# A planned order chosen anew: early norms on GpSimd, mask products in two turns only

## The chip, the cores and the metric

One core of a Trainium2 chip runs the kernel. The metric is the device time in microseconds of one execution; the kernel before takes 620.43 us in the median of three runs (619.21 to 622.95).

## What is computed

Three layers follow one another, all in float32, for 4 batches of 576 tokens with 8 heads of width 64 (512 channels):

- windowed attention: `scores = q k^T / 8`, masked to the last 64 positions, softmax, `attn v`;
- a gated layer: `h = relu(x w_in)`, split in `u` and `v`; `v` is normalised over its channels; `gated = u * (w_spatial v_n + b)`; then `gated w_out`;
- a token and channel mixer: `u = x + w_tok2^T relu(w_tok1^T x)`, `out = u + relu(u w_ch1) w_ch2`.

A full float32 product is made of three faster ones: each operand is split in a high part (a cast) and a low part (the rest), and high·high, high·low and low·high are summed in PSUM. The weights arrive as 64-bit floats and are turned into float32 on the chip (a scaling on ScalarE, two integer operations on VectorE) before they are split.

## The kernel before

The first part of the kernel, up to about 220 us, is attention and most of the gated layer. It runs in 18 **turns** of 128 query rows (two turns collect the tail rows of two batches, 0 and 9). Nothing in it is ordered by hand: the function `plan` lists steps, each with an engine, a rank, a cost in us, the steps that it follows (`after`), and the buffers that it takes and gives (`take`, `give`); class `Steps` plays a simple model of the core in Python while the program is built. It takes next, among the steps that could start soonest, the one of the lowest rank, and writes its instructions. The engines then run in that written order, each with its own queue, and wait on semaphores for what the other engines owe. The costs therefore fix the order and nothing else.

The steps of turn n, with the names that this text uses:

- **Lq, Lv**: SyncE issues the loads of queries and keys (640 KB; 768 KB in the tail turns) and values (512 KB). Two turns' buffers each.
- **S** (`scores`, PE): 32 small products into two PSUM banks `sp` (four exist). In turns below `MASK_PE`, here 6, two bf16 products of an identity with the mask (L278, step **K** in this text) go ahead of them, so that the mask is already in the sum.
- **M** (`smax`, DVE, in two halves g of four heads): with the mask in the sum one reduction gives the maxima (L294, L301). In the other turns four custom instructions (L297) subtract from the mask, write the result to SBUF and leave the maxima, and the PSUM bank is free after M, not after X.
- **X** (`sexp`, ACT): four exponentials per half (L306), from PSUM or from SBUF, as M left them.
- **N** (`snorm`, DVE): sum plus epsilon, reciprocal (L314, L315, 128x4 each), and the multiplication of the half by it (L316, 128x512).
- **T** (PE): four transposes (L488) into a bank `sp`; **C** (ACT): the copy to SBUF (L489).
- **V** (`att_pv`, PE), then **xh** (ACT) and **xl** (DVE): the two parts of the layer's input.
- **v** (PE, 12 products) with its norm and split (`norm_parts`: relu and casts on ACT, statistics and low part on DVE, the inverse root on GpSimd, L375 and L376); after each third turn four **u** products; **s**, the spatial products, with their DVE eviction **G** (L406).

The weight `w_in` comes in eight pieces of 512 KB, four for v and four for u (`w_part`): load (SyncE) into a part of U, **wd** (ACT, L136) into a PSUM bank `mm`, **wo** (DVE, L439 and L440), **wh** (ACT, L443), **wl** (DVE, L445). The piece holds one of only three banks `mm` from wd to wl; the products v, u, s and one V of a pair use the same three. The first v needs all four v pieces.

SyncE issues nearly all loads in one queue. The first fourteen stand in a fixed list: q0, wv0, q1, wv1, v0, wv2, wv3, q2, v1, wu0, q3, wu1, wu2, wu3 (q: a turn's Lq, v: its Lv).

Work of the later layers (the pieces of `w_ch2`, names `craw`, `cx`, `raw`, `scr`; those of `w_out`, names `craw`, `val`) has the highest rank numbers and fills what the engines have left. `w_out` may start only after the last xl. Behind the plan, the rest of the kernel is written in order, with loads `k<-in_w_t` on the same SyncE queue.

Of the kernel before, what the change touches and what calls it, by code (L numbers as in the profile page):

```python
# [22 lines left out]
SCALE = 0.125  # L23
WN = 256
XW = 384
MASK_PE = 6
PB = 3
REST = 4
PAD = 0
PAIRS = 4  # L30
DOWN = 2.0 ** -112
SIGN = -2.0 ** 32

# [5 lines left out]
class Steps:  # L39
# [4 lines left out]

    def __init__(self, **room):
        self.room = {k: [0.0] * n for k, n in room.items()}
        self.clock, self.done, self.open, self.lines = {}, {}, [], {}
# [50 lines left out]
def tile_kernel(ctx, tc, qT, kT, kE, v, w_in, wsT, b_sp, w_out, w_t1, w_t2, w_c1, w_c2, outT):  # L98
# [328 lines left out]
    def w_part(raw, src, hi, lo, cols):  # L427
# [16 lines left out]
        yield  # L444
        nc.vector.tensor_tensor(out=lo, in0=v3, in1=f(hi), op=ALU.subtract)  # L445

    def wu_part(ft):
        fs = slice(128 * ft, 128 * ft + 128)
        return w_part(U[:, ft, :1024], w_in[:, fs].rearrange("(k p) c -> p k c", p=P), wi_h[:, :, fs], wi_l[:, :, fs], 128)
# [10 lines left out]
    def plan():  # L460
# [11 lines left out]
        def attend(n):  # L472
# [8 lines left out]
            def turned(g):  # L481
# [7 lines left out]
                copies[n, g] = lambda: nc.scalar.copy(out=PT[0][:, 4 * g:4 * g + 4, :], in_=pt)  # L489

            for g in range(2):
                S.add(("M", n, g), "DVE", 1 + n / 100, 0.95, lambda g=g: smax(n, g), after=[("S", n)], give=free * (n >= MASK_PE))
                S.add(("X", n, g), "ACT", 2 + n / 100, 1.65, lambda g=g: sexp(n, g), after=[("M", n, g)], give=free * (n < MASK_PE), hold=1.54)
                S.add(("N", n, g), "DVE", 1 + n / 100, 1.15, lambda g=g: snorm(n, g), after=[("X", n, g)], hold=1.05)
                S.add(("T", n, g), "PE", 1 + n / 100, 0.65, lambda g=g: turned(g), after=[("N", n, g)], take=free + ["PT"] * (g == 0), give=["pb"] * g, line=("T", n), hold=0.45)
                S.add(("C", n, g), "ACT", 1, 0.6, lambda g=g: copies.pop((n, g))(), after=[("T", n, g)], give=free, hold=0.49)
# [6 lines left out]

        def score(n, after, line):
            S.add(("S", n), "PE", 0, 1.2 + 0.6 * (n < MASK_PE), lambda: scores(n), after=after + [("Lq", n), "ident"],
                  take=[] if after else ["sp", "sp", "pb"], give=["qk"], hold=1.0 + 0.6 * (n < MASK_PE), line=line)

        def block(ns):

# [14 lines left out]
            take = ["xo"] + ["mm"] * (len(ns) - 1) + ["XT"] * sum(its[m][1] % 3 == 0 for m in ns) + ["sp", "sp", "pb"] * len(ahead)  # L524
            for m in ns:
                S.add(("V", m), "PE", 0, 1.25, lambda m=m: product(m), after=[("V", n)] if m > n else need,
                      take=take if m == n else [], give=["v", "PT"], hold=1.05, line=("B", n))
            for m in ahead:
                score(m, [("V", n)], ("B", n))
            for m in ns:  # L530
                S.add(("xh", m), "ACT", 0, 0.6, lambda m=m: xhigh(m), after=[("V", m)], hold=0.49)
                S.add(("xl", m), "DVE", 0, 0.7, lambda m=m: xlow(m), after=[("xh", m)], give=["mm" if m > n else "xo"], hold=0.6)

        def xhigh(n):
            p, i = its[n]
# [9 lines left out]
        def v_work(p, i):  # L545
# [12 lines left out]
            def part():  # L558
                next(g["it"], 0)

            S.add(("v", n), "PE", 10, 2.9, product, after=[("xl", n)] + [("wl", "v", k) for k in range(4)], take=["mm"], hold=2.75, line="work")
            S.add(("R", n), "ACT", 1.5, 0.6, relu, after=[("v", n)], take=["vf"], give=["mm"], hold=0.49)
            S.add(("bn", n), "DVE", 2, 0.9, part, after=[("R", n)])
            S.add(("rs", n), "POOL", 0, 1.0, part, after=[("bn", n)])
            S.add(("ts", n), "DVE", 2, 0.56, part, after=[("rs", n)])
            S.add(("hi", n), "ACT", 4, 0.6 if i else 2.2, part, after=[("ts", n)])
            S.add(("lo", n), "DVE", 3, 0.7 if i else 1.3, part, after=[("hi", n)], give=["vf"])

        def u_work(p, c, ft):
            g = {}  # L570

            def product():
                g["ps"] = bank(psmm, "mm")
                uv_u_mm(p, c, ft, g["ps"])

            S.add(("u", p, c, ft), "PE", 10, 2.25, product, after=[("xl", 9 * p + 3 * c + k) for k in range(3)] + [("wl", "u", ft)],
                  take=["mm"], give=["XT"] * (ft == 3), hold=2.09, line="work")
            S.add(("E", p, c, ft), "ACT", 1.5, 0.5 if c == 2 else 0.72, lambda: uv_u_out(p, c, ft, g["ps"]), after=[("u", p, c, ft)], give=["mm"])

        def s_work(b, d, c0):  # L580
            p = b // 2
# [2 lines left out]
            def product():  # L584
# [4 lines left out]
            S.add(("s", b, d, c0), "PE", 10, 2.0, product, after=tiles + [("ws", k, c0) for k in range(6)], take=["mm"], hold=1.86, line="work")  # L589
            S.add(("G", b, d, c0), "DVE", 0.5, 0.47, lambda: spatial_out(b, d, c0, g["ps"]),  # L590
                  after=[("s", b, d, c0)] + [("E", p, c, d) for c in range(2 + b % 2)], give=["mm"], hold=0.4)

        def w_load(kind, k):
            it = (wv_part if kind == "v" else wu_part)(k)

            def part():
                next(it, 0)

            S.add(("wL", kind, k), "SP", 0, 0, part, hold=0.47, kb=512, line="SP")
            S.add(("wd", kind, k), "ACT", 1.8 if kind == "v" else 2.5, 0.7, part, after=[("wL", kind, k)], take=["mm"], hold=0.6)  # L600
            S.add(("wo", kind, k), "DVE", 0.8 if kind == "v" else 2.5, 1.25, part, after=[("wd", kind, k)])
            S.add(("wh", kind, k), "ACT", 1.8 if kind == "v" else 2.5, 0.6, part, after=[("wo", kind, k)], hold=0.49)
            S.add(("wl", kind, k), "DVE", 0.8 if kind == "v" else 2.5, 0.7, part, after=[("wh", kind, k)], give=["mm"], hold=0.6)

        def ws_load(k, c):
            rows = P if k < 4 else 64
# [7 lines left out]
            S.add(("wh", k, c), "ACT", 3, 0.45, part, after=[("Lw", k, c)], hold=0.35)  # L614
            S.add(("ws", k, c), "DVE", 2.5, 0.45, part, after=[("wh", k, c)], give=["raw"], hold=0.38)

        def fetch_words(name, src, after, rank, line):

# [92 lines left out]
        for fn, *a in ((load_queries, 0), (w_load, "v", 0), (load_queries, 1), (w_load, "v", 1), (load_values, 0), (w_load, "v", 2), (w_load, "v", 3),  # L711
                       (load_queries, 2), (load_values, 1), (w_load, "u", 0), (load_queries, 3), (w_load, "u", 1), (w_load, "u", 2), (w_load, "u", 3)):
            fn(*a)
        for k in (0, 1):
            score(k, [], ("S", k))
# [594 lines left out]
```

## Time and profile before

| | |
|---|---|
| runs | 619.21, 620.43, 622.95 us |
| profiled execution | 621.39 us, span 619.5 us |
| granted TensorE clock, mean | 0.991 |
| PE busy | 600.2 us (97%) |
| DVE busy | 472.6 us (76%) |
| ACT busy | 352.7 us (57%) |
| POOL (GpSimd) busy | 114.7 us (19%) |
| DMA | 108.05 MB, mean 174 GB/s |

Busy shares are means over the whole span. The page's slices of 15.5 us show PE at four tenths in the first slice and at nine or more in nearly all others, and the clock in tenths at 8 in the first two slices and 9 or more (full) after. So what the first turns do has to be read in its own stretch. An idle time is named with the engine that ended it.

### The profile page before, as it was taken

How to read it: one execution, taken by the hardware profiler on the slowest of the kernel's cores; microseconds unless marked ns; L12 is line 12 of the kernel's file. 1: busy time of each engine (PE TensorE's matmuls, PEld its weight loads, DVE VectorE, ACT ScalarE, POOL GpSimd, SP SyncE). 2: the span in 40 equal slices, each digit the busy share in tenths (PEclk: the TensorE clock that was granted, in tenths of full speed). 3: DMA queues.
4: the chain of work that ended last, by engine and by line, in shares of the span. 5: the costliest groups of instructions: out<-in, count | busy, mean ns of one | idle time of the engine just before them, and what ended most of it. 6: DMA issues, size and time to landing. Idle time of an engine off the chain costs nothing.

```text
span 619.5 us, 12149 instructions
## 1 busy us (share of the span) xinstructions
PE 600.2 (97%) x4396; PEld 560.6 (90%) x4396; DVE 472.6 (76%) x1066; ACT 352.7 (57%) x889; POOL 114.7 (19%) x145
## 2 busy tenths in 40 slices
PE   4999999999999989999999999999999999999997
PEld 2678899889988989788988999999999999999997
DVE  5998878968888836586278778888875989866982
ACT  5996786766777532674344454546443557544540
POOL 3000202302422200041025212140011140011320
PEclk8899999999999999999999999999999999999999
DMA  8956356866565652415200524665534674444752
GB/s 325 342 187 188 124 198 228 262 225 223 203 203 180 229 179 69 137 57 167 84 34 35 170 69 169 221 224 168 184 126 173 230 234 159 153 137 170 237 197 77
DMA packets 49812, 108.05 MB, mean 174 GB/s; under 512 B 4948, under 2 KB 17496, under 8 KB 49752
## 3 DMA queue, kind: packets, MB, share of 16 engines
q1 hardware_dynamic: 49752, 107.27, 51.2%
q8 instruction: 35, 0.57, 0.4%
q14 instruction: 25, 0.20, 0.1%
HBM read 86.81 MB, written 20.45 MB: 173 GB/s over the span
## 4 chain that ended last, share of the span: by engine, by line
PE 62%; DVE 4%; DMA 4%; ACT 2%; issue 1%; POOL 0%; ACTq 0%
PE A L1167 19%; PE mm L183 13%; PE mm L955 12%; PE A L955 9%; PE A L183 6%; DMA scr<-raw 3%; PE A L873 1%; DMA craw<-in_w_out 1%; PE A L1251 1%; DVE pb L297 1%; DVE raw L689 0%; ACT raw L686 0%; DVE pb L316 0%; DVE st L372 0%; DVE hid L949 0%
## 5 line engine op out<-in xcount | busy, mean ns | idle before, releaser
L1167 PE MATMUL A<-room,w 128*128 128x384 f32 x720 | 131.1, 335 | 0.7 <-DVE U L1203 0.7
L1167 PEld LDWEIGHTS A<-room,w 128*128 128x128 f32 x720 | 125.1, 188 | 2.1 <-DVE U L1203 1.0
L1161 ACT CAST room<-hid 128x384 fp32r<-128x384 f32 x120 | 61.3, 513 | 48.9 <-PE A L1167 37.5
L1162 DVE TENSOR_TENSOR room<-hid,room 128x384 fp32r<-128x384 f32 x120 | 71.9, 625 | 13.9 <-ACT room L1161 12.2
L949 POOL TENSOR_TENSOR hid<-hid 128x384 f32<-128x384 f32 x36 | 44.2, 1239 | 202.8 <-DVE hid L949 160.0
L183 PE MATMUL mm<-ws,room 128*128 128x288 f32 x416 | 61.0, 297 | 1.6 <-DVE U L406 1.5
L183 PEld LDWEIGHTS mm<-ws,room 128*128 128x128 f32 x416 | 56.7, 188 | 2.6 <-DVE U L406 2.1
L980 ACT ACTIVATE hid<-hid 128x384 f32<-128x384 f32 x54 | 28.1, 525 | 42.4 <-DVE hid L983 42.4
L983 DVE TENSOR_TENSOR hid<-A,hid 128x384 f32<-128x384 f32 x54 | 29.5, 554 | 24.7 <-PE A L955 18.4
L306 ACT ACTIVATE pb<-pb,nm 128x128 f32<-128x128 f32 x96 | 37.2, 392 | 2.8 <-DVE nm L297 2.8
L955 PE MATMUL mm<-room,sh 128*128 128x384 f32 x144 | 37.2, 334 | 0.0
L183 PE MATMUL mm<-xh,wi_h 128*128 128x384 f32 x96 | 33.2, 346 | 0.0
L183 PE MATMUL mm<-xh,wi_l 128*128 128x384 f32 x96 | 32.2, 336 | 0.0
L183 PE MATMUL mm<-xl,wi_h 128*128 128x384 f32 x96 | 32.2, 335 | 0.0
L1192 DVE TENSOR_TENSOR U<-A,U 128x384 f32<-128x384 f32 x42 | 21.9, 551 | 11.1 <-PE A L1167 6.5
L183 PE MATMUL mm<-gh,wo_h 128*128 128x512 f32 (+1 forms) x80 | 30.2, 378 | 0.0
L183 PE MATMUL mm<-gl,wo_h 128*128 128x512 f32 (+1 forms) x80 | 29.6, 370 | 0.2 <-DVE gl L855 0.2
L813 POOL TENSOR_TENSOR k<-k 128x256 f32<-128x256 f32 x12 | 9.7, 832 | 107.1 <-ACT gh L854 59.4
L183 PE MATMUL mm<-gh,wo_l 128*128 128x512 f32 (+1 forms) x80 | 29.5, 369 | 0.0
L855 DVE TENSOR_TENSOR gl<-U,gh 128x512 fp32r<-128x512 f32 (+1 forms) x20 | 13.3, 667 | 21.1 <-ACT gh L854 21.0
L488 PE MATMUL sp<-ident,pb 128*128 128x128 f32 x144 | 21.7, 284 | 7.0 <-DVE pb L316 3.0
L170 ACT CAST sh<-k 128x1024 fp32r<-128x1024 f32 x18 | 18.9, 1050 | 15.7 <-PE mm L955 5.9
(181 smaller groups left out, 1546.0 us busy)
## 6 DMA issues: line engine op xcount, KB each, us to landing
w<-scr SPq DMA_DIRECT2D x63, 512.0 KB, 4.1
scr<-raw SPq DMA_DIRECT2D x48, 256.0 KB, 3.5
k<-sums SPq DMA_DIRECT2D x18, 512.0 KB, 3.8
kk<-in_kT SPq DMA_DIRECT2D x16, 384.0 KB, 5.5
craw<-in_w_c SPq DMA_DIRECT2D x24, 256.0 KB, 3.7
qq<-in_qT SPq DMA_DIRECT2D x18, 256.0 KB, 5.5
va<-in_v SPq DMA_DIRECT2D x18, 256.0 KB, 4.4
vb<-in_v SPq DMA_DIRECT2D x18, 256.0 KB, 4.6
```

The costliest lines, as they stand in the source:

```text
L170: nc.scalar.copy(out=hi, in_=x)
L183: nc.tensor.matmul(o, a, c, start=(i == 0), stop=(i == n - 1))
L306: nc.scalar.activation(out=pb[:, h, :], in_=scs[g][:, h - 4 * g, :] if mk is None else pb[:, h, :], func=AF.Exp, scale=SCALE if mk is None ...
L488: nc.tensor.transpose(pt[:, h, :], pb[:, 4 * g + h, :], ident)
L949: eng.tensor_tensor(out=out, in0=a, in1=b, op=ALU.subtract)
L955: nc.tensor.matmul(o, a, m, start=first and i == 0, stop=i == len(todo) - 1, skip_group_check=True)
L980: nc.scalar.activation(out=o, in_=src, func=AF.Relu)
L983: nc.vector.tensor_tensor(out=o, in0=a, in1=b, op=ALU.add)
L1161: nc.scalar.copy(out=oh, in_=blk[j])
L1162: nc.vector.tensor_tensor(out=ol, in0=blk[j], in1=f(oh), op=ALU.subtract)
L1167: nc.tensor.matmul(acc[d], a, m, start=(first and j == 0 and i == 0), stop=(last and j == NJ - 1 and i == 2), skip_group_check=True)
L1192: nc.vector.tensor_tensor(out=at, in0=src, in1=at, op=ALU.add)
```

## The change

- `MASK_PE` goes from 6 to 2: turns 2 to 5 drop the two mask products on PE and take the other form of M and X.
- N is cut in two steps: **I** (DVE, L314 and L315) and N, the multiplication. In turns 0 to 4 (`EARLY`) N runs on GpSimd.
- Six of the copies C go from ACT to DVE: half 0 of turn 0, and half 1 of turns 3 to 7.
- Two u weight pieces, 1 and 2 (`PU`), are worked in place in U (SBUF) without a bank `mm`; their wl runs on GpSimd.
- The fourteen loads are issued in another order: wv1, q0, q1, wv3, v0, q2, wv2, wv0, q3, v1, wu0, wu1, wu3, wu2.
- All ranks of DVE, ACT and T steps are new numbers; some costs are changed, and the model now charges PE a small time where it goes from one kind of product to another (`SWITCH`).

```diff
-MASK_PE = 6
+MASK_PE = 2
+EARLY = range(0, 5)
+CD0 = range(0, 1)
+CD1 = range(3, 8)
+PU = (1, 2)
+ORDER = (3, 0, 2, 6, 4, 7, 5, 1, 10, 8, 9, 11, 13, 12)
+RANK = dict(M=0.84, X=3.6, I=-0.18, N=0.7, T=2.63, C=2.91, xh=1.31, xl=0.53, R=3.61, bn=0.54, ts=3.3, hi=5.45, lo=1.36, E=2.39, G=5.62, av=3.1, dv=-0.14, au=3.06, du=0.79, aw=3.29, dw=4.82)
...
+            if eng == "PE":
+                shape = SHAPE.get(name[0])
+                at += SWITCH.get((self.shape, shape), 0.0)
+                self.shape = shape
...
         nc.vector.reciprocal(out=rs, in_=rs)
-        nc.vector.tensor_tensor(out=pb[:, hs, :], in0=pb[:, hs, :], in1=rs.unsqueeze(2).to_broadcast([P, w, 128]), op=ALU.mult)
+        yield
+        eng = nc.gpsimd if n in EARLY else nc.vector
+        eng.tensor_tensor(out=pb[:, hs, :], in0=pb[:, hs, :], in1=rs.unsqueeze(2).to_broadcast([P, w, 128]), op=ALU.mult)
...
+    def wu_pool(ft):
+        fs = slice(128 * ft, 128 * ft + 128)
+        raw = U[:, ft, :1024]
+        words = raw.rearrange("p (a c w) -> p a c w", a=4, w=2)
+        x, y, low = words[:, :, :, 1], words.bitcast(I32)[:, :, :, 1], words.bitcast(I32)[:, :, :, 0]
+        hi, lo = wi_h[:, :, fs], wi_l[:, :, fs]
+        nc.sync.dma_start(...)
+        yield
+        down(x, y)
+        yield
+        nc.vector.tensor_scalar(out=y, in0=y, scalar1=3, scalar2=None, op0=ALU.logical_shift_left)
+        nc.vector.scalar_tensor_tensor(out=y, in0=low, scalar=29, in1=y, op0=ALU.logical_shift_right, op1=ALU.bitwise_or)
+        yield
+        nc.scalar.copy(out=hi, in_=x)
+        yield
+        nc.gpsimd.tensor_tensor(out=lo, in0=x, in1=f(hi), op=ALU.subtract)
...
+                def copy():
+                    out = PT[0][:, 4 * g:4 * g + 4, :]
+                    if n in (CD0, CD1)[g]:
+                        nc.vector.tensor_copy(out=out, in_=pt)
+                    else:
+                        nc.scalar.copy(out=out, in_=pt)
...
-                S.add(("M", n, g), "DVE", 1 + n / 100, 0.95, ...)
-                S.add(("X", n, g), "ACT", 2 + n / 100, 1.65, ...)
-                S.add(("N", n, g), "DVE", 1 + n / 100, 1.15, ...)
+                S.add(("M", n, g), "DVE", RANK["M"] + n / 100, 0.9, ...)
+                S.add(("X", n, g), "ACT", RANK["X"] + n / 100, 1.8 if n >= MASK_PE else 1.6, ...)
+                S.add(("I", n, g), "DVE", RANK["I"] + n / 100, 0.25, ...)
+                S.add(("N", n, g), "POOL" if early else "DVE", RANK["N"] + n / 100, 1.45 if early else 0.8, ...)
...
+        for fn, *a in (loads[i] for i in ORDER):
```

## Rows read from the trace of the kernel before

**Rows 1.** stretches: PE, PEld, DVE, ACT, POOL busy us; clock, DMA share, GB/s
```profile
0.00:20.00 20.00, 11.37 (x134) 7.65 (x138) 12.55 (x26) 11.68 (x35) 4.71 (x19) 0.77 0.93 342
20.00:45.00 25.00, 22.56 (x285) 16.99 (x278) 23.90 (x61) 24.58 (x96) 1.26 (x4) 0.98 0.76 256
45.00:200.00 155.00, 152.82 (x1575) 138.87 (x1574) 129.67 (x464) 114.00 (x383) 31.50 (x52) 1.00 0.60 202
200.00:240.00 40.00, 38.38 (x269) 37.72 (x268) 24.39 (x57) 15.34 (x34) 5.19 (x8) 1.00 0.49 163
```

**Rows 2.** waits of TensorE up to 240 us: releaser, us in total, times, longest
```profile
PE sp L488 <- DVE pb L316: 3.0, 3, 1.5
...
PE mm L183 <- DVE U L406: 1.5, 1, 1.5
```

**Rows 3.** timeline of TensorE, 17 to 42 us: start, us, operation, wait
```profile
17.86 1.03 PE L278 MATMUL sc<-msk,ident 128*128 128x512 bf16 x2
...
20.75 1.24 PE L183 MATMUL mm<-wi_h,xh 128*128 128x512 f32 x4
...
23.64 0.61 PE L278 MATMUL sc<-msk,ident 128*128 128x512 bf16 x2
...
24.17 1.10 PE L283 MATMUL sc<-kk,qq 64*64 64x128 f32 x32
...
41.67 1.20 PE L183 MATMUL mm<-wi_h,xh 128*128 128x512 f32 x4 [0.97 <-DVE wi_l L445]
```

**Rows 4.** window of the half clock, columns as in Rows 1
```profile
10.60:20.90 10.30, 7.52 (x75) 5.38 (x75) 10.03 (x21) 8.14 (x26) 0.00 (x0) 0.50 1.04 387
```

**Rows 5.** timeline of ScalarE, 5 to 20 us: first and last two weight pieces
```profile
6.82 0.63 ACT L136 ACTIVATE mm<-U 128x512 f32<-128x512 f32 x1 [4.82 <-DMA U<-in_w_in]
...
13.56 1.19 ACT L136 ACTIVATE mm<-U 128x512 f32<-128x512 f32 x2
```

**Rows 6.** timeline of VectorE, 5 to 20 us
```profile
10.42 0.69 DVE L316 TENSOR_TENSOR pb<-pb,rs 128x512 f32<-128x512 f32 x1
...
11.03 0.68 DVE L445 TENSOR_TENSOR wi_l<-mm,wi_h 128x512 fp32r<-128x512 f32 x1
```

**Rows 7.** timeline of ScalarE, exponentials from PSUM, then from SBUF
```profile
19.11 0.36 ACT L306 ACTIVATE pb<-sc,nm 128x128 f32<-128x128 f32 x1
19.46 0.36 ACT L306 ACTIVATE pb<-sc,nm 128x128 f32<-128x128 f32 x1
...
58.91 0.39 ACT L306 ACTIVATE pb<-pb,nm 128x128 f32<-128x128 f32 x1
59.29 0.39 ACT L306 ACTIVATE pb<-pb,nm 128x128 f32<-128x128 f32 x1
```

**Rows 8.** groups by line and shape, 0 to 200 us: busy us, mean ns
```profile
L316 DVE TENSOR_TENSOR pb<-pb,rs 128x512 f32<-128x512 f32 x36 | 24.9, 692 | 1.2
...
L297 DVE CUSTOM_DVE_ANT_0 pb<-sc,msk 128x128 f32<-128x128 f32 x96 | 21.1, 286 | 0.0
...
L294 DVE TENSOR_REDUCE mx<-sc 128x4 f32<-128x512 f32 x12 | 8.2, 684 | 7.1 <-PE sc L283 7.1
```

**Rows 9.** source view of L949: minimum, median and maximum ns on GpSimd
```profile
L949 POOL TENSOR_TENSOR hid<-hid x36: 1011/1306/1391, 363.9 to 590.5; 128x384 f32<-128x384 f32 x36
```

**Rows 10.** timeline of VectorE and GpSimd: a pair alone, and beside GpSimd
```profile
122.98 0.76 DVE L689 TENSOR_TENSOR raw<-cx,raw 128x256 fp32r<-128x256 f32 x2
...
162.25 0.74 POOL L679 TENSOR_TENSOR cy<-cx 128x256 f32<-128x256 f32 x1
...
162.43 1.72 DVE L689 TENSOR_TENSOR raw<-cx,raw 128x256 fp32r<-128x256 f32 x2
```

**Rows 11.** chain of waits, VectorE and TensorE at the plan's end
```profile
215.39 7.40 DMA craw<-in_w_out
...
221.02 0.29 DVE L630 TENSOR_SCALAR val<-val 128x256 int32<-128x256 int32 x1 [3.86 <-ACT val L136]
...
222.19 1.06 PE L183 MATMUL mm<-ws,room 128*128 128x288 f32 x6 [1.48 <-DVE U L406]
```

More of the change, by code (lines that the diff above doesn't have):

```diff
@@ L46, in __init__ @@
         self.room = {k: [0.0] * n for k, n in room.items()}
[L47 removed]
+        self.clock, self.done, self.open, self.lines, self.shape = {}, {}, [], {}, None
         self.pad, self.queue, self.lands = 0, 0.0, [0.0] * 8
@@ L488, in turned @@
                     nc.tensor.transpose(pt[:, h, :], pb[:, 4 * g + h, :], ident)
-                copies[n, g] = lambda: nc.scalar.copy(out=PT[0][:, 4 * g:4 * g + 4, :], in_=pt)
-            for g in range(2):
[L492 to L496, printed above, removed]
+                def copy():
[4 more added lines that the diff above has]
+                        nc.scalar.copy(out=out, in_=pt)
+                copies[n, g] = copy
+            for g in range(2):
+                S.add(("M", n, g), "DVE", RANK["M"] + n / 100, 0.9, lambda g=g: smax(n, g), after=[("S", n)], give=free * (n >= MASK_PE))
+                S.add(("X", n, g), "ACT", RANK["X"] + n / 100, 1.8 if n >= MASK_PE else 1.6, lambda g=g: sexp(n, g), after=[("M", n, g)], give=free * (n < MASK_PE), hold=1.54 if n >= MASK_PE else 1.37)
+                early = n in EARLY
+                norm = snorm(n, g)
+                S.add(("I", n, g), "DVE", RANK["I"] + n / 100, 0.25, lambda norm=norm: next(norm), after=[("X", n, g)], hold=0.2)
+                S.add(("N", n, g), "POOL" if early else "DVE", RANK["N"] + n / 100, 1.45 if early else 0.8, lambda norm=norm: next(norm, 0), after=[("I", n, g)], hold=1.4 if early else 0.72)
+                S.add(("T", n, g), "PE", RANK["T"] + n / 100, 0.65, lambda g=g: turned(g), after=[("N", n, g)], take=free + ["PT"] * (g == 0), give=["pb"] * g, line=("T", n), hold=0.45)
+                S.add(("C", n, g), "DVE" if n in (CD0, CD1)[g] else "ACT", RANK["C"], 0.6, lambda g=g: copies.pop((n, g))(), after=[("T", n, g)], give=free, hold=0.49)
         def load_queries(n):
@@ L505, in score @@
             S.add(("S", n), "PE", 0, 1.2 + 0.6 * (n < MASK_PE), lambda: scores(n), after=after + [("Lq", n), "ident"],
-                  take=[] if after else ["sp", "sp", "pb"], give=["qk"], hold=1.0 + 0.6 * (n < MASK_PE), line=line)
+                  take=[] if after else ["sp", "sp", "pb"], give=["qk"], hold=0.98 + 0.6 * (n < MASK_PE), line=line)
         def block(ns):
@@ L526, in block @@
                 S.add(("V", m), "PE", 0, 1.25, lambda m=m: product(m), after=[("V", n)] if m > n else need,
-                      take=take if m == n else [], give=["v", "PT"], hold=1.05, line=("B", n))
+                      take=take if m == n else [], give=["v", "PT"], hold=0.92, line=("B", n))
             for m in ahead:
@@ L559, in part @@
                 next(g["it"], 0)
-            S.add(("v", n), "PE", 10, 2.9, product, after=[("xl", n)] + [("wl", "v", k) for k in range(4)], take=["mm"], hold=2.75, line="work")
-            S.add(("R", n), "ACT", 1.5, 0.6, relu, after=[("v", n)], take=["vf"], give=["mm"], hold=0.49)
-            S.add(("bn", n), "DVE", 2, 0.9, part, after=[("R", n)])
+            S.add(("v", n), "PE", 10, 2.95, product, after=[("xl", n)] + [("wl", "v", k) for k in range(4)], take=["mm"], hold=2.83, line="work")
+            S.add(("R", n), "ACT", RANK["R"], 0.6, relu, after=[("v", n)], take=["vf"], give=["mm"], hold=0.49)
+            S.add(("bn", n), "DVE", RANK["bn"], 0.9, part, after=[("R", n)])
             S.add(("rs", n), "POOL", 0, 1.0, part, after=[("bn", n)])
-            S.add(("ts", n), "DVE", 2, 0.56, part, after=[("rs", n)])
-            S.add(("hi", n), "ACT", 4, 0.6 if i else 2.2, part, after=[("ts", n)])
-            S.add(("lo", n), "DVE", 3, 0.7 if i else 1.3, part, after=[("hi", n)], give=["vf"])
+            S.add(("ts", n), "DVE", RANK["ts"], 0.56, part, after=[("rs", n)])
+            S.add(("hi", n), "ACT", RANK["hi"], 0.6 if i else 2.2, part, after=[("ts", n)])
+            S.add(("lo", n), "DVE", RANK["lo"], 0.7 if i else 1.3, part, after=[("hi", n)], give=["vf"])
         def u_work(p, c, ft):
@@ L574, in product @@
                 uv_u_mm(p, c, ft, g["ps"])
-            S.add(("u", p, c, ft), "PE", 10, 2.25, product, after=[("xl", 9 * p + 3 * c + k) for k in range(3)] + [("wl", "u", ft)],
-                  take=["mm"], give=["XT"] * (ft == 3), hold=2.09, line="work")
-            S.add(("E", p, c, ft), "ACT", 1.5, 0.5 if c == 2 else 0.72, lambda: uv_u_out(p, c, ft, g["ps"]), after=[("u", p, c, ft)], give=["mm"])
+            S.add(("u", p, c, ft), "PE", 10, 2.3, product, after=[("xl", 9 * p + 3 * c + k) for k in range(3)] + [("wl", "u", ft)],
+                  take=["mm"], give=["XT"] * (ft == 3), hold=2.17, line="work")
+            S.add(("E", p, c, ft), "ACT", RANK["E"], 0.5 if c == 2 else 0.72, lambda: uv_u_out(p, c, ft, g["ps"]), after=[("u", p, c, ft)], give=["mm"])
         def s_work(b, d, c0):
@@ L588, in s_work @@
             tiles = [("lo", 9 * p)] + [("lo", 9 * p + 1 + 4 * (b % 2) + m) for m in range(4)]
-            S.add(("s", b, d, c0), "PE", 10, 2.0, product, after=tiles + [("ws", k, c0) for k in range(6)], take=["mm"], hold=1.86, line="work")
-            S.add(("G", b, d, c0), "DVE", 0.5, 0.47, lambda: spatial_out(b, d, c0, g["ps"]),
+            S.add(("s", b, d, c0), "PE", 10, 2.05, product, after=tiles + [("ws", k, c0) for k in range(6)], take=["mm"], hold=1.93, line="work")
+            S.add(("G", b, d, c0), "DVE", RANK["G"], 0.47, lambda: spatial_out(b, d, c0, g["ps"]),
                   after=[("s", b, d, c0)] + [("E", p, c, d) for c in range(2 + b % 2)], give=["mm"], hold=0.4)
         def w_load(kind, k):
-            it = (wv_part if kind == "v" else wu_part)(k)
+            pool_does = kind == "u" and k in PU
+            it = (wv_part if kind == "v" else wu_pool if pool_does else wu_part)(k)
             def part():
                 next(it, 0)
+            bank_of = [] if pool_does else ["mm"]
+            a, d = RANK["a" + kind], RANK["d" + kind]
+            eng = "POOL" if pool_does else "DVE"
             S.add(("wL", kind, k), "SP", 0, 0, part, hold=0.47, kb=512, line="SP")
[L600 to L603, printed above, removed]
+            S.add(("wd", kind, k), "ACT", a, 0.75, part, after=[("wL", kind, k)], take=bank_of, hold=0.6)
+            S.add(("wo", kind, k), "DVE", d, 1.25, part, after=[("wd", kind, k)])
+            S.add(("wh", kind, k), "ACT", a, 0.6, part, after=[("wo", kind, k)], hold=0.49)
+            S.add(("wl", kind, k), eng, d, 1.5 if pool_does else 0.7, part, after=[("wh", kind, k)], give=bank_of, hold=1.4 if pool_does else 0.6)
         def ws_load(k, c):
```

15 lines of the change are left out of this document (9 added, 6 removed).

## The prediction

> **What bounds the kernel now.** I read the busy times by stretch first. TensorE is the bound: over the span it idles 619.5 - 600.2 = 19.3 us. By stretch [rows 1] it idles 8.6 us of the first 20, 2.4 of the next 25, 2.2 of the 155 up to 200 us and 1.6 up to 240. The change touches only the planned part, which ends near 220 us, so what it can win is this idle time, the time in which PE works at the half clock, and PE work that falls away. Second, who is short where PE idles. From 20 to 45 us ScalarE is busy 24.6 of 25 us and VectorE 23.9 [rows 1]: both are full, and a relief of one alone meets the other. From 45 to 200 us VectorE is at 129.7 of 155 us and PE hardly waits. Third, PE's waits [rows 2]: of those that an order can change, the longest are transposes that wait for the norm's multiplication (3.0 us in three waits, over the whole plan) and 1.5 us at the plan's end. Fourth, the start itself in the timelines. ScalarE gets its first weight piece at 6.82 us and the last two together at 13.56 [rows 5]; the first v product starts at 20.75 and the third at 41.67, after a wait of 0.97 us for a weight's low part, that is for a bank [rows 3]. From 10.6 to 20.9 us the granted clock is 0.50, the lower level of 1.2 GHz, after a stretch in which PE mostly waited [rows 4].
>
> **The change part by part**, against the profiled execution's 621.39 us, which lies 0.96 above the median of 620.43.
>
> *Masks.* Eight products leave PE, two in each of turns 2 to 5. At full clock a pair takes from 23.64 to 24.17 = 0.53 us [rows 3]; three pairs stand behind the first v product, in work that PE has to do anyway: **-1.6 us**. Turn 2's pair at 17.86 runs at half clock ahead of it and is counted with the start. What replaces them: four custom instructions of 21.1/96 = 0.22 us for a reduction of 0.68 and its scaling [rows 8], about even on VectorE; and the exponentials now read SBUF and start 0.38 us apart where those from PSUM start 0.35 apart [rows 7], 32 x 0.03 = 1.0 us more on ScalarE. The score banks come free one exponential step earlier. Gain at most the 2.1 us of four pairs, at least 0 if PE only waits longer for something else.
>
> *The multiplication on GpSimd.* VectorE spends 11.03 - 10.42 = 0.61 us on one [rows 6]; ten leave: -6.1 us. On GpSimd a subtraction of 384 columns took 1.01 to 1.39 us [rows 9] and one of 256 took 0.74 [rows 10]; for 512 columns that gives 1.28 (straight line through the quick ones) to 1.85 (the slow one in proportion). I take 1.4. So each half reaches its transposes 0.7 to 1.2 us later, and the small inverse roots of the v norm queue behind up to two such instructions, 2.8 us; the spatial products that need them come tens of us later and cover that. The two low parts on GpSimd take 2 x 0.6 us off VectorE and give back the bank `mm` that they held; the 0.97 us wait at 41.67 is of that kind.
>
> *Copies.* Four of the six that move fall before 45 us: about +4 x 0.6 us on VectorE (the planner's own cost; the multiplication of the same 512 columns takes that), as much off ScalarE. A copy on VectorE waits for PE's transposes, and behind it stand the next turn's M and I and any weight step; if the transposes are late, all of these are.
>
> *In-place pieces.* ScalarE and VectorE read and write every second word in SBUF instead of PSUM. No row shows that; the nearest is the shift of a later weight, 256 columns in SBUF in 0.29 us [rows 11], so I take no difference, with 0.3 us per instruction either way (six instructions: 1.8 us).
>
> Together VectorE loses -6.1 - 1.2 + 2.4 = **-4.9 us** before 45 us, and ScalarE about -2.4 + 1.0 = **-1.4 us**.
>
> *Loads.* The list has the same fourteen. wv1's one DMA goes ahead of q0's two on SyncE's queue: 524 KB at 0.39 MB/us [rows 4] make turn 0's scores some 1.3 us later and the first weight about as much earlier than 6.82. q2's two DMAs go ahead of the last two v pieces, and q2 needs a buffer that turn 0's scores hold, so these two pieces' issues also wait for those scores. 655 KB in front of the last piece cost 1.7 us: 13.56 becomes about 15.3. From the second of that pair (14.2, half of the 1.19 us later) to the first v product (20.75) it took 6.6 us before, with VectorE full; four multiplications fewer (2.4 us) and a VectorE that starts 1.3 us earlier make it 4 to 5: **v starts at about 19.4**, 1.3 us earlier, between 18.6 and 22. Part of it then still runs at half clock if the clock rises at 20.9 as before: +0.6. Start: **-0.7 us**, ends -2.1 and +1.5.
>
> *20 to 45 us.* 2.4 us of idle. Turn 1's maxima stood behind the weights on VectorE; now they come earlier, and ScalarE's gaps of the first 20 us (8.3 us) can take its exponentials. I take two thirds: **-1.6 us**; ends -2.4 and +2 (the later transposes).
>
> *45 to 200 us.* 2.2 us of idle, all of it waits that the written order makes; the new ranks shuffle them. I take **-0.6**, ends -1.8 and +2. *200 to 240 us:* **0**, ends -1.6 and +4 (second rival).
>
> The sum is -1.6 - 0.7 - 1.6 - 0.6 = -4.5 us: 616.9 for such an execution, **615.9 us** in the median.
>
> **Rivals.**
>
> *All of it is won.* The order fits the chip: v starts at 18.6 and nothing waits after it. The sum of the good ends is -2.1 - 2.1 - 2.4 - 1.8 = -8.4, or 612.0 us in the median. For it: PE's idle time after 20 us comes in few, single waits, each with a named cause. Against: ScalarE is as full as VectorE and is relieved by 1.4 us only.
>
> *Given back at the plan's end.* PE lost 1.5 us there because a spatial eviction stood in VectorE's queue behind a conversion of `w_out` that waited 3.9 us for ScalarE, and ScalarE for that weight's transfer; the chain has one of 7.4 us there [rows 11]. That chain hangs on transfers and on the filler work, not on PE. If PE comes 4.5 us earlier and the chain only 1.5 us, 3 us of the gain turn into a longer wait there: 618.9 us. For it: the filler lives on what VectorE has left, and that is 25 us from 45 to 200, where the change frees nothing. Against: the `w_out` steps may start as soon as the last low part is made, which moves with PE.
>
> *GpSimd and VectorE block each other: slower.* Two low parts of 256 columns took 0.76 us on VectorE alone and 1.72 beside a GpSimd instruction of 0.74 [rows 10]. Twelve new GpSimd instructions of 1.4 us make 16.8 us in which this can happen, nearly all before 45 us, where VectorE has no slack. If half of it is lost, 8.4 us, VectorE is 3.5 us behind instead of 4.9 ahead; with the late end of the start (+1.5) and the masks' -1.6 that is +3.4, or 623.8 us. It decides once VectorE loses more than 4.9 us. Against: what VectorE runs there takes one operand from PSUM (M, the v weights' steps, xl, the copies) or is 4 columns wide (I); two SBUF operands of size occur in the two in-place pieces, in the v norm's low part and in the spatial weights alone. The Trainium skill (SBUF — State Buffer, Who interferes with whom) states the rule behind this: a VectorE instruction with two SBUF inputs and a GpSimd one that reads SBUF use one port, and the later one stands still until the other is done; the trace agrees, with 1.72 for 0.76. If each of the twelve met such an instruction at its beginning, the rule would give 16.8 us lost and 632 us.
>
> That the change does not do what it says is hardly a rival: masks and engines are plain in the code.
>
> **How the numbers follow.** Forecast 0.48, all won 0.16, given back 0.22, blocked 0.14. A measurement of this kernel can tell about 1%, 6.2 us, from no change: under 614.2 is faster, over 626.6 slower. The forecast's own range is 612.5 to 619 and a third of it lies under 614.2 (0.16); with 0.15 of the all-won case and 0.02 of the third that makes 0.33 faster. Slower takes 0.06 of the last rival, whose lost share can be larger than half, and 0.01 of the rest. Same is 0.60. The range, 611 to 622, leaves out the far end of either side, about one in ten each.
>
> **What would show it.** Right: the first L183 product before 20 us; TensorE's idle time from 20 to 45 us under 1.2 us; no `sc<-msk` products after turn 1; VectorE with gaps before 45 us; no wait for `wi_l` at the third v. The clock back at full level by 21 us, else the start gains nothing. Wrong by the second rival: a wait on L406 near 215 us of over 3 us. Wrong by the third: L384, L440 or L314 at twice their time beside GpSimd's multiplication, and PE waiting at its transposes. The prediction fails altogether if the new order makes a wait that no row here shows, for example VectorE standing at a copy for PE while PE stands for VectorE.

## The result and the profile after

The changed kernel takes **626.87 us** in the median of five runs (626.37 to 631.45), the kernel before 620.43 in five of the same session: a ratio of 1.0113 [1.0071, 1.0155]. The profiled execution has a span of 624.8 us. It was to be 4.5 us faster; it is 6.4 us slower, above the upper end of the range.

Where the time went is told by one instruction, the first product with `w_out` behind the plan, in TensorE's timeline. Before, it starts at 241.27 us:

```profile
241.27 0.40 PE L183 MATMUL mm<-gh,wo_h 128*128 128x512 f32 x1
```

After (L195 is the former L183):

```profile
246.55 0.40 PE L195 MATMUL mm<-gh,wo_h 128*128 128x512 f32 x1
```

That is 5.28 us later, and what follows it takes 378.3 us in both. All of the loss lies in the planned part. Its stretches, columns as in [rows 1]:

```profile
0.00:20.00 20.00, 11.17 (x122) 7.56 (x123) 11.38 (x32) 10.67 (x40) 8.72 (x23) 1.00 0.84 310
20.00:45.00 25.00, 22.52 (x301) 18.89 (x298) 23.99 (x99) 24.75 (x86) 11.60 (x15) 1.00 0.78 263
45.00:200.00 155.00, 148.90 (x1544) 134.52 (x1543) 126.20 (x461) 113.14 (x382) 30.94 (x49) 0.99 0.61 207
200.00:240.00 40.00, 37.03 (x247) 35.84 (x247) 22.31 (x52) 15.63 (x33) 5.31 (x9) 1.00 0.49 154
```

The clock of 1.00 in the first row is no gain: 32 score products take 1.99 us at 7.17 and 15.59 us and 1.10 us at 23.53, so PE works at half pace there, as it does in most of that stretch before. Against [rows 1], TensorE's idle time is the same up to 45 us (8.8 and 2.5 for 8.6 and 2.4 us), grows from 2.2 to 6.1 us between 45 and 200, and from 1.6 to 3.0 behind. The products that both kernels run can be set side by side, at three places where PE has done the same ones in both but for the eight mask products: at the eighth spatial product (98.28 for 100.80 us) the changed kernel is still 2.5 us ahead; at the 17th u product (179.96 for 179.80) it is level; at the 21st (205.29 for 201.08) it is 4.2 behind. So 2.7 us go at 100 to 150 us and 4.1 at 180 to 192. The waits of TensorE between 45 and 240 us, all of them (releaser, us in total, times, longest):

```profile
PE sp L520 <- DVE pb L330: 4.5, 5, 2.2
PE mm L195 <- DVE U L420: 3.0, 1, 3.0
PE sp L520 <- DVE rs L326: 1.5, 3, 0.6
```

The rows of before that answer to them are in [rows 2]. PE waits at its transposes (L520), for the norm's steps on VectorE. Those are not slow themselves: they wait for exponentials (VectorE by 1.72 us at 100.94), and these came late. ScalarE's timeline before the waits of 103 to 105 us:

```profile
95.76 0.45 ACT L148 ACTIVATE cx<-craw 128x256 f32<-128x256 f32 x1
98.92 0.44 ACT L148 ACTIVATE cx<-craw 128x256 f32<-128x256 f32 x1 [2.71 <-DMA craw<-in_w_c]
99.27 0.39 ACT L318 ACTIVATE pb<-pb,nm 128x128 f32<-128x128 f32 x1
```

A scaling of a `w_ch2` piece, which nobody needs soon, stands in the written order ahead of the exponentials (L318) and waits 2.71 us for its load. Exponentials, transposes, V, v and u all stand behind that one load. On PE it comes out as two waits, 0.47 us at 103.97 and 0.91 at 105.50. SyncE's queue shows what stands ahead of the load:

```profile
92.24 0.38 SPq L269 DMA_DIRECT2D va<-in_v  x1
92.72 0.42 SPq L270 DMA_DIRECT2D vb<-in_v  x1
93.24 0.42 SPq L668 DMA_DIRECT2D craw<-in_w_c  x1
```

It is issued right behind 512 KB of values and lands near 98.9, 5.7 us after its issue; the median of the 24 loads of `w_ch2` pieces is 3.5 us. The planner's own formula gives a piece of 256 KB 1.3 + 256/330 + 0.8 = 2.9 us on an idle queue, and some 3.4 us with these values ahead of it (an estimate by the formula, with the issue times shown).

The chain that ended last shows filler again from 167 us on, here a load and a send of a finished half:

```profile
167.90 4.88 DMA craw<-in_w_c
...
177.05 4.78 DMA scr<-raw
181.85 0.41 ACT raw L733
182.26 3.12 ACT pb L318 x16
```

The send is the smaller part: ScalarE's own waits for sends are 0.63 and 0.24 us there. PE is on time with these scores (175.20 us for 175.03 before), but the first exponential comes 3.4 us later. ScalarE's and VectorE's timelines in between:

```profile
172.80 0.43 ACT L148 ACTIVATE cx<-craw 128x256 f32<-128x256 f32 x1 [2.68 <-DMA craw<-in_w_c]
177.59 0.44 ACT L148 ACTIVATE cx<-craw 128x256 f32<-128x256 f32 x1 [2.33 <-POOL cy L726]
178.54 0.55 DVE L392 TENSOR_SCALAR vf<-vf,mv,rstd 128x512 f32<-128x512 f32 x1 [1.58 <-POOL rstd L390]
182.16 0.40 ACT L318 ACTIVATE pb<-pb,nm 128x128 f32<-128x128 f32 x1
```

Before (L306 is the later L318):

```profile
178.76 0.40 ACT L306 ACTIVATE pb<-pb,nm 128x128 f32<-128x128 f32 x1 [0.19 <-DVE nm L297]
```

Behind the late load stand the filler's sums on GpSimd (`cy`, 174.16 to 177.55 us), behind these an inverse root of the v norm, for which VectorE waits 1.58 us, and behind that the maxima: they start at 181.06 us, where before they started at 178.43.

What it leads to on PE, with the window of the granted clock behind it (columns as in [rows 1]):

```profile
186.51 0.84 PE L520 MATMUL sp<-ident,pb 128*128 128x128 f32 x4 [2.20 <-DVE pb L330]
187.91 1.09 PE L520 MATMUL sp<-ident,pb 128*128 128x128 f32 x4 [0.55 <-DVE rs L326]
```

```profile
186.78:190.19 3.41, 2.86 (x13) 2.49 (x12) 3.31 (x12) 3.41 (x18) 1.17 (x2) 0.50 0.00 0
```

After the idle time of 2.20 us the clock was granted at 0.50, the level of 1.2 GHz, for 3.41 us: the next u product took 0.7 us more. And at the plan's end the case of [rows 11] comes back, with a longer wait of PE. ScalarE, VectorE and PE there:

```profile
224.39 0.43 ACT L148 ACTIVATE val<-craw 128x256 f32<-128x256 f32 x1 [3.92 <-DMA craw<-in_w_out]
```

```profile
225.18 0.42 DVE L678 SCALAR_TENSOR_TENSOR val<-craw,val 128x256 int32<-128x256 int32 x1
225.52 0.45 DVE L420 TENSOR_TENSOR U<-mm,U 128x288 f32<-128x288 f32 x1
```

```profile
226.02 1.99 PE L195 MATMUL mm<-ws,room 128*128 128x288 f32 x13 [2.96 <-DVE U L420]
```

The spatial eviction (L420) stands behind the conversion of a `w_out` piece whose load took 6.22 us, and PE, out of banks, waits 2.96 us. That costs 1.1 us net (5.28 less 4.2), since before lost some 2 us there, 1.48 of them in its wait [rows 11].

### The profile page after: what moved, and what is told of

It is laid out like the page before. It is cut to its first block, busy times and chain, and to the rows that moved or that the text cites. A ratio compares the mean times of both kernels' runs of the same rounds, so it can differ in the third digit from the quotient of the medians.

```text
span 624.8 us, 12200 instructions
## 1 busy us (share of the span) xinstructions
PE 600.0 (96%) x4388; PEld 561.5 (90%) x4388; DVE 469.5 (75%) x1108; ACT 351.9 (56%) x883; POOL 128.5 (21%) x157
## 4 chain that ended last, share of the span: by engine, by line
PE 68%; DMA 11%; DVE 10%; ACT 8%; issue 2%; SPq 1%; POOL 1%; ACTq 0%; DVEq 0%; POOLq 0%
PE A L1215 19%; PE mm L195 16%; PE mm L1003 12%; PE A L1003 9%; PE A L195 6%; DMA craw<-in_w_c 4%; ACT pb L318 4%; DMA craw<-in_w_out 3%; DMA scr<-raw 2%; PE A L921 1%; DVE raw L736 1%; DMA U<-in_w_in 1%; PE A L1299 1%; PE sc L295 1%; PE sp L520 1%
## 5 line engine op out<-in xcount | busy, mean ns | idle before, releaser
L195 PE MATMUL mm<-ws,room 128*128 128x288 f32 x416 | 60.9, 297 | 3.0 <-DVE U L420 3.0
L195 PEld LDWEIGHTS mm<-ws,room 128*128 128x128 f32 x416 | 56.7, 188 | 3.9 <-DVE U L420 3.2
L318 ACT ACTIVATE pb<-pb,nm 128x128 f32<-128x128 f32 x128 | 49.8, 392 | 2.2 <-DVE nm L309 2.2
L195 PE MATMUL mm<-xh,wi_h 128*128 128x384 f32 x96 | 33.6, 350 | 0.0
L195 PE MATMUL mm<-xh,wi_l 128*128 128x384 f32 x96 | 32.5, 338 | 0.0
L195 PE MATMUL mm<-xl,wi_h 128*128 128x384 f32 x96 | 32.5, 338 | 0.0
L520 PE MATMUL sp<-ident,pb 128*128 128x128 f32 x144 | 23.2, 294 | 9.3 <-DVE pb L330 4.5
L195 PE MATMUL mm<-gh,wo_h 128*128 128x512 f32 (+1 forms) x80 | 30.2, 378 | 0.0
L520 PEld LDWEIGHTS sp<-ident,pb 128*128 128x128 f32 x144 | 17.4, 149 | 14.1 <-ACT pb L318 6.8
L195 PE MATMUL mm<-gl,wo_h 128*128 128x512 f32 (+1 forms) x80 | 29.6, 370 | 0.2 <-DVE gl L903 0.2
L195 PE MATMUL mm<-gh,wo_l 128*128 128x512 f32 (+1 forms) x80 | 29.6, 370 | 0.0
```

Of the source, the lines that this page charges most:

```text
L195: nc.tensor.matmul(o, a, c, start=(i == 0), stop=(i == n - 1))
L318: nc.scalar.activation(out=pb[:, h, :], in_=scs[g][:, h - 4 * g, :] if mk is None else pb[:, h, :], func=AF.Exp, scale=SCALE if mk is None ...
```

## The experiments

**Theory**: the change itself is worth something, and the new written order loses more than that after 100 us, because filler work that waits for its own loads stands ahead of the attention chain. **Rivals**: the cut norm or GpSimd's part makes the chain late; or the new order wins nothing and the filler only fills its gaps. The columns of the table are the ratio to the kernel before on the same chip, the start of the first `w_out` product, and PE's idle time from 45 to 200 and from 200 to 240 us. The kernel before took 620.43 to 622.82 us beside these runs, so rows are best compared by the ratio or by the first `w_out` product.

| kernel | median us | ratio [95%] | first w_out | idle 45–200 | 200–240 |
|---|---|---|---|---|---|
| before | 620.43 | 1 | 241.27 | 2.2 | 1.6 |
| after | 626.87 | 1.0113 [1.0071, 1.0155] | 246.55 | 6.1 | 3.0 |
| a1 masks alone | 622.27 | 1.0010 [0.9991, 1.0029] | 241.38 | 4.0 | 0.5 |
| a2 after, old ranks | 623.93 | 1.0024 [0.9992, 1.0056] | 245.09 | 5.7 | 0.0 |
| a3 after, filler in bulk | 641.43 | 1.0306 [1.0262, 1.0350] | 263.00 | 12.9 | 4.0 |
| a4 after, norm whole | 628.65 | 1.0115 [1.0065, 1.0165] | 247.24 | 6.2 | 0.7 |
| c1 after, no filler loads | 614.47 | 0.9876 [0.9854, 0.9897] | 233.84 | 0.0 | 0.0 |
| c2 before, no filler loads | 618.89 | 0.9944 [0.9922, 0.9966] | 237.76 | 1.3 | 0.0 |
| b2 after, norm on VectorE | 637.35 | 1.0227 [1.0198, 1.0256] | 258.52 | 8.3 | 1.8 |
| c3 after, landing 2 us later | 620.07 | 0.9966 [0.9950, 0.9982] | 240.38 | 0.0 | 4.0 |
| c4 before, landing 2 us later | 630.08 | 1.0126 [1.0100, 1.0152] | 250.93 | 1.5 | 3.8 |
| e1 after, craw alone 2 us later | 620.12 | 0.9960 [0.9945, 0.9976] | 240.31 | 4.5 | 0.1 |
| e2 after, landing 1 us later | **615.16** | **0.9888 [0.9872, 0.9904]** | 234.65 | 0.0 | 0.0 |
| e3 before, landing 1 us later | 625.99 | 1.0067 [1.0055, 1.0079] | 243.01 | 0.0 | 4.6 |

### Parts of the change (a1 to a4, b2)

a1, the masks alone, in the kernel before:

```diff
-MASK_PE = 6
+MASK_PE = 2
```

> The kernel before with MASK_PE = 2 alone; everything else, ranks and loads included, as before, planned anew. My forecast's masks term: the first product of w_out starts 1.6 to 2.1 us before the 241.3 us of before, 618.3 to 618.8 us. Rival (any new order loses to late waits what it wins, whatever the part): 620 to 624 us.

No change, as the rival said. The 2.1 us of products are gone, but the planner lays a new order, and it has two new waits at 46 and 48 us (2.06 and 1.34 us). Its waits of PE up to 60 us hold this row:

```profile
PE sp L488 <- ACT pb L306: 2.1, 1, 2.1
```

So even the simplest part is given back by the order that is laid for it.

a2, the change with the ranks of before:

```diff
-RANK = dict(M=0.84, X=3.6, I=-0.18, N=0.7, T=2.63, ...)
+RANK = dict(M=1, X=2, I=1, N=1, T=1, ...)
```

> The changed kernel with the ranks of before in RANK (I and N with N's old rank), all else as changed. If the new ranks make the late waits at 103, 125, 144 and 182 to 188 us: 617 to 620 us, TensorE idle from 60 to 200 us back to about 2 us. If they come from the rest (norm cut in two, shorter costs, loads): 625 to 628 us, idle still 5 us or more.

It lies between the two ranges and cannot be told from the kernel before; against the changed kernel it is faster, by 1.5 us at the first `w_out` product and by more in the ratio. PE is busy 19.36 us from 20 to 45 us, where it is 22.52 in the changed kernel: the ranks chosen anew are worth some 3 us there, and lose them again, part of it at the plan's end (no idle time here, 3.0 us there). The late idle time stays at 5.7 us. The new ranks alone are not what makes it.

a3 holds the filler steps from a pair's V to the next pair's last exponential and writes them then in one lump:

```diff
+        if name[0] == "V" and name[1] in range(4, 16, 2):
+            last = ("X", name[1] + 3, 1)
+        if last and name[0] in fill:
+            held.append((name, fn))
+            continue
...
+        if name == last:
+            out += held
```

> The changed kernel in its own written order, except that the filler of the later layers (the steps of w_ch2 and w_out) is not written between a pair's V and the last exponential of the next pair, but right behind it. Theory 'filler': ScalarE stands in front of the exponentials at filler that waits for its transfers, so the waits at 103, 144 and 182 to 188 us go and the first product of w_out starts 3 to 5 us earlier than 246.5: 622 to 624 us. Rival 'cut norm' (other steps slip between the reciprocal and the multiplication): no change, 626 to 627.5. Rival 'filler is late then': the wait at 221 us grows from 3 us by as much as is won, 626 to 629.

A miss: far slower than the changed kernel, by 16.5 us at the first `w_out` product. The lump now stands ahead of norm and copies instead of the exponentials, and PE's waits for the norm grow:

```profile
PE sp L539 <- DVE pb L349: 10.1, 5, 3.0
PE sp L539 <- DVE rs L345: 5.7, 2, 3.8
```

It shows how strongly the place of the filler decides, not that my cure was one.

a4 lets I and N run as one step from turn 5 on:

```diff
-... lambda norm=norm: next(norm), ...
+... lambda norm=norm, early=early: (next(norm), early or next(norm, 0)), ...
```

> The changed kernel in its own order, but in turns 5 to 17 the multiplication is written right behind the reciprocal, at the place of step I. Theory 'filler': each late multiplication comes 0.3 to 0.4 us earlier and the waits shrink by no more than that, 625.5 to 626.5 us. Rival 'cut norm': most of the late waits go, 621 to 623 us.

Above both ranges, but not told apart from the changed kernel by the ratio, and with the same late idle time (6.2 for 6.1 us): the rival of the cut norm falls.

b2 takes the multiplications back to VectorE (`EARLY = ()` for `range(0, 5)`).

> The changed kernel with the multiplications of the first five turns back on VectorE; masks, queue order, ranks, cut norm and the two low parts on GpSimd stay, and the planner lays the order anew for it. Theory 1 (the loss is made late, by an order without slack): this part is worth little either way, 625 to 629 us, and the excess of PE before 50 us rises by 0 to 3 us. Rival (GpSimd's multiplications block VectorE's small scalings, 0.71 in place of 0.17 us, and make the plan late): PE's excess before 50 us falls by 2 us or more and the time is 622 to 624.5 us.

Both expectations missed: slower than the changed kernel, by 12.0 us at the first `w_out` product and by some 7 us in the ratio. Its stretches:

```profile
0.00:20.00 20.00, 9.26 (x108) 6.05 (x108) 10.96 (x34) 9.83 (x39) 4.71 (x19) 0.85 0.80 297
20.00:45.00 25.00, 17.08 (x236) 14.18 (x236) 20.90 (x93) 20.13 (x79) 0.00 (x0) 0.78 0.64 209
```

PE stands 7.9 us of the second stretch, one wait of it 4.55 us long, for a copy C that VectorE makes. Taking GpSimd's multiplications back did not help; how much of the loss is theirs and how much the new order's own stays open.

### The filler's loads (c1, c2)

```diff
+                if fixed:
+                    raws[name] = fixed[0]
+                    return
+                raws[name] = stage.tile([P, 512], I32, tag="craw", name="craw", bufs=1)
+                fixed.append(raws[name])
```

> The changed kernel, with every load of a craw tile but the first left out: the scalings of w_ch2 and w_out read the first tile again, so these weights are wrong, and 256 KB less stands in the DMA queues for each; the written order is the same. Theory 1 (the loss is made after 100 us, where a cx scaling that waits for its craw load stands ahead of an exponential on ScalarE): the waits of transposes at 103, 125, 144, 147 and 182 us, about 7 us together, go for the most part, and the first w_out product comes at 241 to 243 us in place of 246.5: 620.5 to 623 us. Rival (the attention chain itself runs late, from the late start, GpSimd's norm and the cut norm, and the filler only fills its gaps): the waits stay within 2 us of 7, 625 to 627 us.

> The kernel before with the same loads left out (w_ch2 and w_out wrong in the same way). It is the scale for the run on the changed kernel. Theory 1: the kernel before has one wait of 1.64 us on this filler, at 218.7 us, and little else: 0 to 2 us faster than before, 618.5 to 621.5 us. Rival: what the loads cost is paid by both kernels alike, so this run gains as much as the changed kernel does without them, 3 us or more if that gains 3.

This shows where the loss is. With the same written order the changed kernel is 12.4 us faster without these loads (626.87 to 614.47; 12.7 by the start of `w_out`), more than the theory asked for; the kernel before gains 3.9 against its own runs there (622.82 to 618.89; 3.5 by the start of `w_out`), so the loads cost both, as the rival of c2 has it in part, and the changed kernel 9 us more. The run takes 31 transfers off the queues along with the waits for them; c3 and e2 below keep all transfers. The changed kernel's stretch, with not one wait of PE behind 45 us:

```profile
45.00:200.00 155.00, 155.00 (x1589) 141.74 (x1589) 133.26 (x479) 117.28 (x392) 37.04 (x56) 1.00 0.52 176
```

The rival, a chain that is late by itself, would have left these waits. And without the loads the change is worth 614.47 to 618.89, 4.4 us to the good.

### The planner's landing times (c3, c4, e1, e2, e3)

The loads stay; only the planner's belief changes, so it writes the order with the scalings farther behind their loads. c3, on the changed kernel:

```diff
-                end = self.queue + 0.8
+                end = self.queue + 0.8 + 2.0 * (name[0] in ("Lc", "Lh"))
```

> The changed kernel, whose planner takes each craw load and each send of w_ch2's halves to land 2.0 us later than it did; nothing else is changed, but the written order is laid anew by it, with the scalings later behind their loads. Theory 1 (the planner takes these loads to land too early, so that scalings stand ahead of exponentials and wait): ScalarE's waits for craw ahead of exponentials shrink to under 1 us each, 621 to 624.5 us. Rival (the landing is not what the order fails by; any new order loses some waits and makes others): 626 to 630 us.

6.2 us come back by the start of `w_out`, and the time is a little under the theory's range. ScalarE's wait for `w_ch2` pieces, 12.5 us in ten times in the changed kernel from 60 to 240 us, is now:

```profile
ACT cx L148 <- DMA craw<-in_w_c: 0.8, 2, 0.6
```

PE has no idle time from 45 to 200 us, but the filler ends later, and the plan's end pays for it:

```profile
235.09 3.46 PE L195 MATMUL mm<-ws,room 128*128 128x288 f32 x13 [3.79 <-DVE U L420]
```

c4, the same edit in the kernel before:

> The kernel before, whose planner takes each craw load and each send of w_ch2's halves to land 2.0 us later; nothing else is changed. Theory 1 (the planner's landing times are too early for either kernel, but the order of the kernel before happened to lose only 4 us by it, as the run without its loads shows): 618 to 622 us, at most 4 us to gain. Rival (the later landing is good in itself, as much as the 6.8 us that it gave the changed kernel): 613 to 616 us.

Neither: 630.08 us. The stretch up to 200 us is better than before (1.5 us idle), the end much worse (most of this wait lies behind 240 us, outside the table's column):

```profile
244.91 2.53 PE L183 MATMUL mm<-ws,room 128*128 128x288 f32 x9 [8.44 <-DVE U L406]
```

e1 has 2.0 us for the craw loads alone.

> The changed kernel, planner with 2.0 us later landing for the craw loads alone, not for the sends. With both late, the waits for craw ahead of exponentials went (12.5 to 0.8 us), and 5.5 us were lost at 229 us, where the last sends of w_ch2's halves come late behind the last s products. Theory 1: it is the craw loads' landing that the early waits hang on, so 60 to 225 us stays without idle; the plan ends earlier than with both late, 615 to 620 us. Rival (the sends' landing matters as much, through the raw buffers ahead of the exponentials): waits for scr<-raw of over 1.5 us stand ahead of exponentials, 622 to 626 us.

The time is at the upper edge of the theory's range, the way is partly the rival's: craw no longer waits, the plan's end is clean, but ScalarE now waits for sends, 13.1 us in eleven times, and PE idles 4.5 us.

e2 has 1.0 us for both (`+ 1.0 *` in the line of c3).

> The changed kernel, planner with both kinds landing 1.0 us later in place of 2.0. The scalings waited up to 2.7 us for craw in the changed kernel. Theory 1 (the planner's landing is early by up to 2.7 us): half of it is mended, 620 to 624 us, with one or two waits of 1 to 2 us left ahead of exponentials; less is lost at the plan's end than with 2.0. Rival (any new order draws its waits anew): anywhere from 614 to 630 us, with waits that don't shrink with the allowance.

**615.16 us**, faster than both kernels: more than the theory allowed, and where it lies in the rival's wide span it has none of the waits that the rival asked for. PE's stretches behind 45 us:

```profile
45.00:200.00 155.00, 155.00 (x1589) 141.75 (x1589) 130.39 (x469) 114.47 (x386) 34.90 (x53) 1.00 0.61 204
200.00:240.00 40.00, 40.00 (x278) 39.09 (x277) 26.08 (x59) 16.49 (x34) 3.30 (x4) 1.00 0.58 195
```

It starts `w_out` at 234.65 us, 0.8 us behind the kernel without the loads. So the loads can be hidden almost altogether; the changed kernel's order just did not do it.

e3, the same 1.0 us in the kernel before:

> The kernel before, whose planner takes craw loads and sends to land 1.0 us later, which made the changed kernel 1.1% faster than the kernel before (615.2 us, no idle of TensorE from 45 to 225 us). Theory 1 (the later landing pays back what an order loses by waits on this filler, and the kernel before loses little): 617.5 to 621.5 us, so that 2 to 6 us of the 615.2 belong to the change. Rival (the allowance of 1.0 us is what makes the kernel faster, whatever the change): 614 to 617 us. A third outcome, as with 2.0 us on this kernel (630 us, 8.6 us lost at the last s products), would say that each allowance lays another order and that its end decides: 623 us or more.

The third outcome: no idle time from 45 to 200 us here either, then 4.6 us at the plan's end, 625.99 us in all. The allowance isn't good by itself. The first `w_out` product comes 8.4 us later than in e2: 4.6 us are this idle time, some 1.7 a half clock granted from 220.7 us on for 3.41 us of full work (an estimate by half of it), and the rest is about what the eight mask products are worth. Whether an order's end falls well or badly no run says in advance. Nor does any say which part of the change laid the scalings where they hurt: the load order, the copies, the in-place pieces and the changed costs were not tried alone.

## Why the prediction was wrong

**The step that failed** is "*45 to 200 us.* 2.2 us of idle, all of it waits that the written order makes; the new ranks shuffle them. I take -0.6, ends -1.8 and +2". The range's end of +2 was passed: from the eighth spatial product to the 21st u product the changed kernel lost 6.7 us (2.5 ahead to 4.2 behind). 3.9 us are more idle time by the stretches, some 1.4 the half clock (half of the 2.86 us that PE was busy in it, an estimate); the last 1.4 stay open. I bounded the waits of an order that I could not see by the waits of the one that I could. The row for the true bound was there: [rows 11] show a load of 7.40 us and a wait of 3.86 us for it. What such a wait costs hangs on what is queued behind it. ScalarE's waits for pieces of `w_ch2` from 60 to 240 us (us in total, times, longest), before and after:

```profile
ACT cx L136 <- DMA craw<-in_w_c: 8.0, 8, 1.8
```

```profile
ACT cx L148 <- DMA craw<-in_w_c: 12.5, 10, 2.7
```

With the waits for sends (7.8 and 4.9 us) the sums are 15.8 and 17.4 us, nearly alike; what differs is that the changed order puts the long ones ahead of exponentials, maxima and norms that PE needs next. c1, c3 and e2 show that it was this: take the loads away, or write their users later, and the stretch has no idle time at all. The prediction named the outcome in its last lines ("the new order makes a wait that no row here shows") but gave it no chance of its own.

*Masks*, -1.6: right in kind. The products were gone after turn 1, and the changed kernel was 2.5 us ahead at 98 us with the eight mask products as the only difference in what PE had done, about what four pairs are worth (2.6 us with turn 2's at half clock). But a1 shows that they are worth nothing by themselves once the order changes.

*Loads*, -0.7, and *20 to 45 us*, -1.6: nothing came of either. The first v product starts at 26.84 us, not 19.4. Queries 0 now stand behind a weight piece, and PE's first scores wait for them, 2.1 us later than before (timeline of PE):

```profile
7.17 1.99 PE L295 MATMUL sc<-kk,qq 64*64 64x128 f32 x32 [2.17 <-DMA kk<-in_kE]
...
14.54 1.12 PE L520 MATMUL sp<-ident,pb 128*128 128x128 f32 x4 [2.50 <-POOL pb L330]
...
26.84 0.96 PE L195 MATMUL mm<-wi_h,xh 128*128 128x512 f32 x3
```

The term that was mis-sized is the last v weight piece. Its load stood behind q2, as foreseen, but ScalarE scaled it at 20.30 us and not at 15.3, behind exponentials and copies in its written order:

```profile
20.30 0.66 ACT L148 ACTIVATE mm<-U 128x512 f32<-128x512 f32 x1
```

PE does the scores of turns 2 to 4 ahead of v, so the late v costs nothing, and nothing is won. PE's products are at full pace from 19.7 us on, so the sign for the clock came true without a gain. The third v comes at 36.07 for 41.67, without the bank's wait, as foreseen; idle time from 20 to 45 us is 2.5 us and not under 1.2. Even e2, with no wait behind 45 us, has the old idle time up to there (8.9 and 2.4 us): its gain is the masks and the late waits, no more. The agreement of c1 against c2 (4.4 us) with my sum (4.5 us) is therefore luck, one of size alone: by the start of `w_out` it is 3.9 us, the masks and the 1.3 us that c2 still idles.

*GpSimd's multiplication*: it was cheaper than the 1.4 us taken, and VectorE's new room was filled with other steps (23.99 of 25 us busy). Two copies C, not four, fell to VectorE before 45 us (16.05 and 41.83 us).

*Given back at the plan's end*: its wait came, in its place and nearly in its size (2.96 us at 226, for over 3), but there was no gain left to give back.

*GpSimd and VectorE block each other*: the lock is there, in small. VectorE's timeline with GpSimd's multiplication of 16.27 us beside it:

```profile
15.75 0.16 DVE L326 TENSOR_SCALAR rs<-sm 128x4 f32<-128x4 f32 x1
...
16.62 0.72 DVE L326 TENSOR_SCALAR rs<-sm 128x4 f32<-128x4 f32 x1
...
17.46 0.66 DVE L459 TENSOR_TENSOR wi_l<-mm,wi_h 128x512 fp32r<-128x512 f32 x1
```

```profile
16.27 1.04 POOL L330 TENSOR_TENSOR pb<-pb,rs 128x512 f32<-128x512 f32 x1 [1.78 <-DVE rs L327]
17.69 1.04 POOL L330 TENSOR_TENSOR pb<-pb,rs 128x512 f32<-128x512 f32 x1 [0.38 <-DVE rs L327]
```

A step of 128x4 (sum plus epsilon, L326) takes 0.16 us alone and 0.72 where it meets GpSimd's instruction, and ends with it; the low part at 17.46, with one operand in PSUM, runs on beside the next one. I had counted these 4-column steps as safe. Four of them (0.64 us at 13.88, 0.72, 0.71 at 18.04, 0.42 at 28.18) and one in-place conversion (1.67 us at 34.42, for 0.69) cost VectorE about 2.8 us before 45 us, over half of the 4.9 at which this rival decides. It did not decide: PE's idle time up to 45 us is that of before, and b2, without these multiplications on GpSimd, is slower, though in an order of its own. The 1.72 us of [rows 10] stood beside two GpSimd instructions, the one of 0.74 us and one of 0.92 at 162.94, not beside one. The Trainium skill (SBUF — State Buffer, Who interferes with whom) says that a VectorE `tensor_scalar` can take the port pair shared with GpSimd too, and that a single SBUF input outside those modes does not contend. The trace agrees, with the first by 0.72 for 0.16 us, with the second by the low part's 0.66.

## What to carry to other kernels

Where a planner fixes the order of in-order engines, a change is two things: what it saves, and a new order. Price the order by the longest transfer that filler work can wait for, standing ahead of the critical chain, and not by the waits that the old order happens to have. Test the two apart: the same order with the filler's loads left out shows what the change is worth. A planner's landing times are then worth several tries, on each kernel by itself: with 0, 1.0 and 2.0 us more the changed kernel took 627, 615 and 620 us, the kernel before 620, 626 and 630.

## What was not expected of the hardware

GpSimd's product of 128x512 with a broadcast operand took 1.04 us in all ten instances, less than the 1.3 to 1.5 us of its two 128x512 subtractions. The granted clock fell to 0.50 for 3.41 us after a single wait of 2.20 us on PE in the middle of full work; the wait of 2.96 us at 226 was followed by no such fall, while one of 1.78 us in e3 was. No run here says what decides.
